# Attention with a token and channel mixer, one core: the product with the values in 64x64 tiles, its key halves added on VectorE, the first queries turned on TensorE, the order table refitted

## The chip, the cores and the metric

One core of a Trainium2 chip runs the kernel. The metric is the device time of one execution in microseconds (us). The clock that the throttle granted to TensorE in the profiled execution was 1.00 of full speed throughout.

## The reference

Causal attention over 4 batches of 12 heads (448 positions, head width 64) feeds a mixer: a small network over the positions of each batch, then one over the channels.

```
scores = q k^T / sqrt(64), causal mask, softmax          # 4 x 12 heads of 448 x 448
x  = softmax @ v, heads side by side                      # 4 x 448 x 768
u  = x + (relu(x^T @ w_tok1) @ w_tok2)^T                  # 448 -> 256 -> 448 over positions
out = u + relu(u @ w_ch1) @ w_ch2                         # 768 -> 1536 -> 768 over channels
```

Everything is float32 in and out.

## The kernel before

The work is cut into 24 pairs of heads, 0 to 23, six to a batch. For each pair the kernel loads keys, queries and values (`load_pair`), turns keys and queries so that the head width lies on the partitions (`prep`), makes the scores and the softmax (`heads`), turns the probabilities so that keys lie on the partitions, multiplies them with the values (`values`) and leaves the result, channels on partitions, in the tile `u`. After every second pair `xturn` turns two slices of `u` for the token network (`tokens`: lines L1350 and L1383); after every batch the channel network follows (`channels`, L1433). The last two batches take the channel network in combined products (L1765, L1836, L1860), 200 us that the change leaves alone.

**Two kinds of pairs.** Pairs 0 to 9 have their probabilities turned by TensorE (`by_tensor`, L1115); they are called flat here. For pairs 10 to 23 a DMA turns them (`by_dma`).

**The product with the values**, `values`, is three TensorE jobs. Two `pv` jobs (L1245) multiply blocks of 128 keys, in float32: the stationary side is 128 keys by 64 channels of one head (the array in two tiles of 128x64, one for each head of the pair), the moving side the probabilities. A `tips` job (L1254) takes the blocks on the causal diagonal that have only 64 keys; it uses the array as four tiles of 64x64, two halves of the keys by two heads. The queries are in seven chunks of 64; some chunks are gathered in the PSUM bank `ps`, the others in the bank `low`, and `evac` copies both parts to `u` (192 + 256 columns). The scores (L1021) use four 64x64 tiles as well.

**First pair.** Keys and queries of pair 0 come in blocks of 32x32 (four DMAs each, keys on SP's queue, queries on ACT's, L940) and VectorE turns both (L988). Pairs 1 to 5 come as they lie (`load_rows`, L892 and L895) and TensorE turns them by products with the identity (`turn_rows`, L916, L910); ACT or VectorE copies the result from PSUM.

**What sets the order.** Each piece of work is a job with a cost for each engine that may run it. A planner that runs while the program is built hands jobs to the engines one after the other: it takes the ready job with the lowest number in the table `PLACES`; `CHOICE` says which engine takes a job that several could do (a ACT, d VectorE, p GpSimd, s SP). Each engine then runs its list in this fixed order. Where TensorE has nothing ready in the plan early on, the planner puts in a filler product (`keep_warm`, L865), whose result nobody reads.

Of the kernel before, what the change touches and what calls it, by code (L numbers as in the profile page):

```python
# [9 lines left out]
F32 = mybir.dt.float32  # L10
# [11 lines left out]
    "load_pair.blocks": {-2: (0, 1), 10: (129, 153), 12: (193, 224), 14: (242, 259), 16: (338, 293), 18: (405, 420),  # L22
        20: (522, 537), 22: (578, 591), 24: (670, 694), 26: (742, 758), 28: (831, 851), 30: (911, 927), 32: (996,
        1006), 34: (1056, 1070), 36: (1141, 1151), 38: (1205, 1220), 40: (1280, 1293), 42: (1333, 1348), 44: (1406,
        1426)},
    "load_pair.load": {0.5: (2,), 2.5: (3,), 4.5: (178,), 6.5: (209,), 8.5: (274,), 10.5: (312,), 12.5: (393,),
        14.5: (453,), 16.5: (490,), 18.5: (558,), 20.5: (615,), 22.5: (704,), 24.5: (773,), 26.5: (822,), 28.5:
        (902,), 30.5: (949,), 32.5: (1047,), 34.5: (1114,), 36.5: (1194,), 38.5: (1241,), 40.5: (1376,), 42.5:
        (1441,), 44.5: (1489,), 46.5: (1531,)},
    "load_pair.upper": {-0.2: (12,), 1.8: (15,), 3.8: (213,), 5.8: (245,), 7.8: (317,), 9.8: (380,), 11.8: (441,),  # L30
        13.8: (505,), 15.8: (519,), 17.8: (592,), 19.8: (651,), 21.8: (727,), 23.8: (821,), 25.8: (859,), 27.8:
        (938,), 29.8: (982,), 31.8: (1077,), 33.8: (1136,), 35.8: (1226,), 37.8: (1269,), 39.8: (1401,), 41.8:
        (1462,), 43.8: (1517,), 45.8: (1561,)},
    "narrow.load": {3.5: (6, 9, 16, 62, 86, 121, 114, 144), 12: (288,), 13: (371,), 14: (445,), 15: (503,), 16:
        (606,), 17: (665,), 18: (755,), 19: (818,), 20: (897,), 21: (974,), 22: (1041,), 23: (1120,), 24: (1191,),
        25: (1254,), 26: (1328,), 27: (1400,), 28: (1463,), 29: (1511,), 30: (1553,), 31: (1599,), 32: (1627,), 33:
        (1660,), 34: (1687,), 35: (1730,)},
    "narrow.size": {3.5: (32, 52, 61, 116, 133, 177, 180, 235), 12: (352,), 13: (413,), 14: (484,), 15: (545,), 16:
        (642,), 17: (705,), 18: (786,), 19: (854,), 20: (932,), 21: (1013,), 22: (1072,), 23: (1153,), 24: (1223,),
        25: (1291,), 26: (1360,), 27: (1437,), 28: (1497,), 29: (1532,), 30: (1584,), 31: (1616,), 32: (1646,), 33:  # L40
        (1676,), 34: (1712,), 35: (1748,)},
    "narrow.shift": {3.5: (37, 56, 73, 125, 142, 183, 186, 263), 12: (359,), 13: (424,), 14: (491,), 15: (554,), 16:
        (646,), 17: (710,), 18: (793,), 19: (863,), 20: (939,), 21: (1019,), 22: (1084,), 23: (1157,), 24: (1227,),
        25: (1295,), 26: (1371,), 27: (1446,), 28: (1503,), 29: (1538,), 30: (1588,), 31: (1621,), 32: (1649,), 33:
        (1678,), 34: (1720,), 35: (1750,)},
    "narrow.join": {3.5: (40, 63, 80, 131, 146, 187, 194, 298), 12: (364,), 13: (436,), 14: (497,), 15: (587,), 16:
        (652,), 17: (724,), 18: (796,), 19: (870,), 20: (948,), 21: (1024,), 22: (1089,), 23: (1161,), 24: (1234,),
        25: (1300,), 26: (1374,), 27: (1450,), 28: (1505,), 29: (1543,), 30: (1590,), 31: (1623,), 32: (1655,), 33:
        (1681,), 34: (1725,), 35: (1755,)},
    "token_weights.<lambda>": {3.5: (44, 69, 85, 135, 150, 191, 201, 303)},  # L50
# [1927 lines left out]
```

## Time and profile before

| what | value |
|---|---|
| runs (3) | 537.52, 537.71, 538.35 us; median 537.71 |
| profiled execution | 538.04 us, of it span 536.2 us |
| TensorE, VectorE, ACT, GpSimd busy | 99%, 80%, 59%, 31% of the span |

The span runs from the first to the last instruction in the trace; 1.84 us of the profiled execution's time lie around it. PE is TensorE's row of products, PEld its loads of the stationary side, DVE is VectorE, POOL is GpSimd. In PE's rows the duration of a product includes its way through the array, so it overlaps with the next one: what a block of products costs is read from the start of its first row to the start of the block behind it. A float32 product shows as two records, so a block of 16 products is "x32" where rows are merged.

### The profile page before, as it was taken

The page shows a single profiled execution, that of the slowest core. Times are in us where ns is not written, and L with a number is a line of the kernel's source. Part 1 is how long each engine was busy: PE and PEld are TensorE (multiplying, and loading weights), DVE is VectorE, ACT ScalarE, POOL GpSimd, SP SyncE. Part 2 cuts the span into 40 slices and gives each one's busy share as a digit, 9 for nine tenths or more (in the row PEclk, how much of TensorE's full clock was granted, in tenths as well). Part 3 has the DMA queues.
Part 4 walks back from the last instruction along what each step waited for, and adds up shares of the span by engine and source line. Part 5 has one row for each costly group of instructions (what it writes and reads, how often), then busy time and mean ns, then how long its engine had stood idle before and what let it go on. Part 6 is the DMA issues. An engine that isn't in the chain of part 4 may idle for free.

```text
span 536.2 us, 12037 instructions
## 1 busy us (share of the span) xinstructions
PE 529.8 (99%) x4391; PEld 460.6 (86%) x4391; DVE 426.4 (80%) x1030; ACT 314.0 (59%) x768; POOL 164.2 (31%) x220
## 2 busy tenths in 40 slices
PE   8999999999999999999999999999999999999997
PEld 4778888888888888888898899999999999999996
DVE  5998899989797999888896679677877848485665
ACT  4998898899888787789784561243232313131300
POOL 2565745444252232332452132140010012321200
PEclk9999999999999999999999999999999999999999
DMA  9966677979999998999969327648213030212147
GB/s 194 198 116 144 152 214 160 215 153 233 207 178 200 225 190 193 205 196 229 210 163 198 115 92 205 131 119 162 88 32 116 7 91 23 87 32 88 31 75 131
DMA packets 221546, 77.72 MB, mean 145 GB/s; under 512 B 195760, under 2 KB 210992, under 8 KB 221488
## 3 DMA queue, kind: packets, MB, share of 16 engines
q1 hardware_dynamic: 207984, 74.90, 63.1%
q10 hardware_dynamic: 13504, 2.07, 2.1%
q8 instruction: 34, 0.56, 0.5%
q14 instruction: 24, 0.20, 0.2%
HBM read 49.15 MB, written 14.94 MB: 120 GB/s over the span
## 4 chain that ended last, share of the span: by engine, by line
PE 94%; SPq 2%; DVE 2%; ACT 1%; DMA 1%; issue 0%; POOL 0%; DVEq 0%; POOLq 0%
PE ps L1433 33%; PE ps L1860 16%; PE ps L1765 12%; PE ps L1021 6%; PE ps L1245 6%; PE ps L1383 6%; PE ps L1350 6%; PE ps L1836 3%; PE ps L1254 1%; PE ps L1115 1%; PE ps L1291 1%; SPq L940 1%; PE ps L865 1%; ACT prob L1055 1%; DMA gh<-in_k_dram 1%; PE ps L910 0%
## 5 line engine op out<-in xcount | busy, mean ns | idle before, releaser
L1500 DVE TENSOR_TENSOR u<-ps,u 128x448 f32<-128x448 f32 x118 | 72.5, 619 | 34.2 <-PE ps L1860 28.0
L1055 ACT ACTIVATE prob<-prob,stat 128x192 f32<-128x192 f32 (+6 forms) x168 | 83.7, 501 | 14.4 <-DVE stat L1043 14.1
L643 POOL TENSOR_TENSOR wl<-wf,wh 128x768 fp32r<-128x768 f32 x26 | 49.5, 1904 | 94.4 <-ACT wh L632 59.4
L1043 DVE CUSTOM_DVE_ANT_0 prob<-ps,mask 128x128 f32<-128x128 f32 (+6 forms) x168 | 63.3, 415 | 7.3 <-PE ps L1021 6.9
L634 POOL TENSOR_SCALAR prob<-prob,stat 128x64 f32<-128x64 f32 (+6 forms) x80 | 43.8, 559 | 55.4 <-DVE stat L1077 42.9
L1433 PE MATMUL ps<-uh,wh 128*128 128x448 f32 x144 | 53.7, 373 | 0.0
L1433 PE MATMUL ps<-gh,wh 128*128 128x448 f32 x144 | 52.9, 367 | 0.0
L1433 PE MATMUL ps<-gh,wl 128*128 128x448 f32 x144 | 52.7, 366 | 0.0
L1433 PE MATMUL ps<-gl,wh 128*128 128x448 f32 x144 | 52.7, 366 | 0.0
L1433 PE MATMUL ps<-uh,wl 128*128 128x448 f32 x144 | 52.7, 366 | 0.0
L1433 PE MATMUL ps<-ul,wh 128*128 128x448 f32 x144 | 52.7, 366 | 0.0
L632 ACT ACTIVATE wh<-wf 128x768 fp32r<-128x768 f32 x27 | 22.5, 846 | 51.2 <-PE ps L1860 25.8
L1021 PE MATMUL ps<-kq,kq 64*64 64x64 f32 (+5 forms) x768 | 45.4, 356 | 0.0
L1021 PEld LDWEIGHTS ps<-kq,kq 64*64 64x64 f32 x768 | 26.6, 133 | 15.5 <-issue 9.6
L1245 PE MATMUL ps<-pt,vraw 128*64 128x128 f32 (+2 forms) x544 | 37.3, 284 | 0.0
L1245 PEld LDWEIGHTS ps<-pt,vraw 128*64 128x64 f32 x544 | 28.2, 137 | 9.8 <-issue 2.1
L1795 DVE TENSOR_TENSOR kq<-kq,ps 128x448 f32<-128x448 f32 x35 | 21.2, 619 | 14.8 <-PE ps L1765 14.2
L1055 ACT ACTIVATION_READ_ACCUMULATOR prob<-prob,stat 128x1 f32 x168 | 32.1, 191 | 0.0
L638 ACT COPY pt<-pt 128x384 uint16<-128x384 uint16 (+3 forms) x41 | 31.6, 830 | 0.8 <-DMA pt<-prob 0.8
L1860 PE MATMUL ps<-u,wh 128*128 128x448 f32 (+1 forms) x110 | 31.0, 363 | 0.0
L1433 PEld LDWEIGHTS ps<-uh,wh 128*128 128x128 f32 x144 | 27.0, 188 | 2.8 <-issue 0.2
L1433 PEld LDWEIGHTS ps<-gl,wh 128*128 128x128 f32 x144 | 27.1, 188 | 2.5 <-DVE gl L1468 0.2
(222 smaller groups left out, 1403.2 us busy)
## 6 DMA issues: line engine op xcount, KB each, us to landing
wraw<-in_moe_w_ch_dram SPq DMA_DIRECT2D x24, 768.0 KB, 5.4
wf<-scratch SPq DMA_DIRECT2D x30, 384.0 KB, 3.1
scratch<-wf SPq DMA_DIRECT2D x24, 384.0 KB, 4.8
vraw<-in_v_dram SPq DMA_DIRECT2D x44, 96.0 KB, 3.4
kq<-in_k_dram SPq DMA_DIRECT2D x60, 56.0 KB, 3.7
kq<-in_q_dram SPq DMA_DIRECT2D x56, 56.0 KB, 2.4
out_dram<-h1l SPq DMA_DIRECT2D x24, 56.0 KB, 2.7
out_dram<-h1h SPq DMA_DIRECT2D x24, 56.0 KB, 2.2
```

Of the source, the lines that this page charges most:

```text
L634: eng[e].tensor_scalar(dst, src, scale, 0.0, op0=ALU.mult, op1=ALU.add)
L643: eng[e].tensor_tensor(dst, a, b, op=ALU.subtract)
L1021: nc.tensor.matmul(scores[n].tile[lanes, to:at], lhsT=qe.tile[LANES[j], c * QC:(c + 1) * QC], rhs=ke.tile[LANES[j], slice(*keys)], start=T ...
L1043: nc.vector.tensor_tensor_reduce(out=part(c, r), in0=ps.tile[:, at:at + wide(c)], in1=mask[:, S - QC:S + P] if c == 2 else mask[:, S - wid ...
L1055: nc.scalar.activation(part(c, r), part(c, r), AF.Exp, bias=stat.tile[:, 0, AT[c]:AT[c] + 1], scale=-1.0, accum_out=stat.tile[:, 1, AT[c]: ...
L1245: nc.tensor.matmul(to, lhsT=s.tile[:, kb, j], rhs=rhs, start=(n in first_of), stop=False)
L1350: nc.tensor.matmul(ps.tile[:, :PART], lhsT=w[:, c, m * P:(m + 1) * P], rhs=x.tile[:, c, :], start=(n == 0), stop=(n == len(work) - 1),)
L1383: nc.tensor.matmul(ps.tile[:, :S], lhsT=h.tile[:, m, o * P:(o + 1) * P], rhs=w[:, m, :], start=(n == 0), stop=(n == 3 * NM - 1),)
L1433: nc.tensor.matmul(ps.tile[:, :S], lhsT=x.tile[:, at_:at_ + P], rhs=y, start=(n == 0 and i == 0), stop=(n + 1 == w[2] and i == 2),)
L1500: eng[e].tensor_tensor(u, ps.tile[:, :S], u, op=ALU.add)
L1765: nc.tensor.matmul(ps.tile[:, :S], lhsT=l()[:, t * P:(t + 1) * P], rhs=r, start=(t == 0 and n == 0), stop=(t == half - 1 and n == 2),)
L1860: nc.tensor.matmul(ps.tile[:, cols], lhsT=l.tile[:, t * P:(t + 1) * P], rhs=r.tile[:, cols], start=(n == 0), stop=(n == 3 * len(fs) - 1),)
```

## The change

1. `values`: each block of 128 keys is split into two halves of 64 keys. All products of this stage now use four 64x64 tiles (two key halves by two heads); the half decides the PSUM bank: keys 0 to 63 add up in `ps`, keys 64 to 127 in `low`. The tips join the second `pv` job. A pair has twice as many products, each with half the depth.
2. `evac`: `nought` copies the whole of `low` (448 columns) to `u`, on ACT or VectorE; then `evac` adds the last 384 columns of `ps` to it, on VectorE.
3. The queries of pair 0 come as they lie, in one DMA of 224 KB on ACT's queue, and are turned on TensorE and copied by ACT or VectorE; VectorE turns only the keys of pair 0.
4. `PLACES` and `CHOICE` have new numbers throughout; two lines of each side stand below.

```
-    "load_rows.load": {0: (7, 4), 2: (10, 23), 4: (30, 45), 6: (68, 79), 8: (105, 91)},
+    "load_rows.load": {-2: (0,), 0: (3, 4), 2: (6, 17), 4: (20, 33), 6: (43, 114), 8: (103, 123)},
-    "load_pair.blocks": {10: "ss", 12: "ss", 14: "ss", 16: "ss"},
+    "load_pair.blocks": {10: "as", 12: "ss", 14: "ss", 16: "ss"},
...
-            {"sp": 535.0 if g < ONCE else 1070.0}, load, holds=[home, s], rank=2.0 * g + RL,
+            {"sp" if g else "act": 535.0 if g < ONCE else 1070.0}, load, holds=[home, s], rank=2.0 * g + RL,
...
+    def lies(g, nm):
+        return nm != "v" and g < WHOLE and (g, nm) != (0, "k")
...
-            if 0 < g < WHOLE and nm != "v":
+            if lies(g, nm):
...
-        def chunks(n, j):
+        def chunks(n, j, half):
 
             if flat_:
-                which, kb, c, step, nq, o, stride = PIECES[n]
-                out = banks[which].tile[LANES[j]].rearrange("p (c q) -> p c q", q=QC)[:, c:c + step * (nq - 1) + 1:step]
-                rhs = pt.tile[:, 1 - j if c in OVER else j, o:o + stride * (nq - 1) + 1:stride]
+                _, kb, c, step, nq, o, stride = PIECES[n]
+                out = banks[half].tile[LANES[j]].rearrange("p (c q) -> p c q", q=QC)[:, c:c + step * (nq - 1) + 1:step]
+                rhs = pt.tile[LANES[half], 1 - j if c in OVER else j, o:o + stride * (nq - 1) + 1:stride]
...
                 for n in part:
-                    for j in range(2):
-                        kb, to, rhs = chunks(n, j)
-                        nc.tensor.matmul(to, lhsT=s.tile[:, kb, j], rhs=rhs, start=(n in first_of), stop=False)
+                    for half in range(2):
+                        for j in range(2):
+                            kb, to, rhs = chunks(n, j, half)
+                            nc.tensor.matmul(to, lhsT=s.tile[LANES[half], kb, j], rhs=rhs, start=n == 0, stop=False)
+                for half, kb, o, c in ENDS if part[0] else ():
...
-                {"pe": 660.0 if part[0] else 718.0}, pv, js + pdone + [prev], [ps, low, s, ends, pt, u], rank, tiled=1
+                {"pe": 878.0 if part[0] else 652.0}, pv, js + pdone + [prev], [ps, low, s, ends, pt, u], rank, tiled=2
...
-        def evac(e):
+        def nought(e):
             if t == 0:
                 make(u, [P, NT, S], F32)
-            copy(e, u.tile[:, t, 3 * QC:], ps.tile[:, 3 * QC:S])
-            copy(e, u.tile[:, t, :3 * QC], low.tile[:, :3 * QC])
+            copy(e, u.tile[:, t], low.tile[:, :S])
+
+        def evac(e):
+            nc.vector.tensor_tensor(u.tile[:, t, QC:], ps.tile[:, QC:S], u.tile[:, t, QC:], op=ALU.add)
...
-        u_ready[b, t] = plan.job(
-            {"act": act_ps(S) + 65.0, "dve": dve1(S) + 70.0}, evac, [prev] + first, [ps, low, u], rank
-        )
+        c = plan.job({"act": act_ps(S), "dve": dve1(S)}, nought, [prev] + first, [low, u], rank)
+        u_ready[b, t] = plan.job({"dve": dve1(S - QC)}, evac, [prev, c], [ps, u], rank)
```

**TensorE's start, before.** After 16 fillers the list goes straight to the scores of pair 0 (L1021); the row behind them turns queries of pair 1 (L916).

```order
L865 MATMUL ps_84<-mask 128x512
L1021 MATMUL ps_140<-kq_121,kq_132 64x448 x2
L1021 MATMUL ps_141<-kq_121,kq_132 64x384 x2
L1021 MATMUL ps_141<-kq_121,kq_132 64x64 x2
L1021 MATMUL ps_149<-kq_121,kq_132 64x320 x2
L1021 MATMUL ps_150<-kq_121,kq_132 64x256 x2
...
L1021 MATMUL ps_149<-kq_121,kq_132 64x128 x2
L916 MATMUL ps_168<-ident,ul_118 64x112 x8
```

The same place in the changed kernel, where the turns are L914, the scores L1022 and the fillers L863. Between the sixth filler and the scores stand the turn of pair 0's queries and three more fillers.

```order
L863 MATMUL ps_84<-mask 128x512
L914 MATMUL ps_116<-ident,ul_96 64x112 x8
...
L863 MATMUL ps_84<-mask 128x512
L1022 MATMUL ps_133<-kq_126,kq_129 64x448 x2
L1022 MATMUL ps_134<-kq_126,kq_129 64x384 x2
...
L1022 MATMUL ps_147<-kq_126,kq_129 64x128 x2
L914 MATMUL ps_161<-ident,uh_113 64x112 x8
L914 MATMUL ps_178<-ident,ul_96 64x112 x8
L914 MATMUL ps_194<-ident,uh_113 64x112 x8
L1022 MATMUL ps_213<-kq_203,kq_206 64x448 x2
```

The first scores now wait for a product and a copy of it, nine fillers instead of 16 stand ahead of them, and three turns without a filler follow.

**TensorE around the values of pair 15, before** (`ps_3116` is the bank `ps`, `ps_3117` the bank `low`; then come scores of pair 17 and, with L1291, the turn of `u` for pairs 14 and 15).

```order
L1433 MATMUL ps_3099<-gh_3048,wl_3014 128x448
L1245 MATMUL ps_3116<-pt_3035,vraw_91 64x256 x2
L1245 MATMUL ps_3117<-pt_3035,vraw_91 64x128 x2
L1245 MATMUL ps_3116<-pt_3035,vraw_91 64x256 x2
L1245 MATMUL ps_3116<-pt_3035,vraw_91 64x128 x2
L1254 MATMUL ps_3116<-pt_3035,vraw_91 64x64 x2
L1254 MATMUL ps_3117<-pt_3035,vend_92 64x64 x2
...
L1021 MATMUL ps_3141<-kq_2941,kq_3005 64x448 x2
...
L1291 MATMUL ps_3169<-ident,u_2587 128x64
```

The same place in the changed kernel (L1247 the blocks, L1250 the tips, L1290 the turn of `u`; `ps_3310` is `ps`, `ps_3311` is `low`).

```order
L1432 MATMUL ps_3289<-gh_3130,wl_3182 128x448
L1247 MATMUL ps_3310<-pt_3200,vraw_91 64x256 x2
L1247 MATMUL ps_3311<-pt_3200,vraw_91 64x256 x2
L1247 MATMUL ps_3310<-pt_3200,vraw_91 64x128 x2
L1247 MATMUL ps_3311<-pt_3200,vraw_91 64x128 x2
...
L1250 MATMUL ps_3310<-pt_3200,vraw_91 64x64 x2
L1250 MATMUL ps_3311<-pt_3200,vend_92 64x64 x2
...
L1022 MATMUL ps_3338<-kq_3179,kq_3223 64x448 x2
...
L1290 MATMUL ps_3373<-ident,u_2786 128x64
```

Each row of the blocks now stands twice, once for each bank, and no row of this piece changes the tile shape between L1247 and the end of the scores.

**VectorE at the same place in the changed kernel** (L1266 is the new add; L1044 the masked scores of the next pair).

```order
L1499 TENSOR_TENSOR u_487<-ps_3289,u_487 128x448
L697 SCALAR_TENSOR_TENSOR wf_3302<-wraw_3219,wf_3302 128x768
L989 STREAM_TRANSPOSE kq_3351<-kq_3262 128x448
L1266 TENSOR_TENSOR u_2786<-ps_3310,u_2786 128x384
L1044 ISA prob_0_85,stat_3369<-ps_3338,mask 128x448
```

The add stands between work for other stages and the masked scores, which wait behind it.

## Rows read from the trace of the kernel before

**Rows 1.** The page, part 1: busy us (share of the span) x instructions.

```profile
PE 529.8 (99%) x4391; PEld 460.6 (86%) x4391; DVE 426.4 (80%) x1030; ACT 314.0 (59%) x768; POOL 164.2 (31%) x220
```

**Rows 2.** The page, part 4: the chain that ended last, by engine.

```profile
PE 94%; SPq 2%; DVE 2%; ACT 1%; DMA 1%; issue 0%; POOL 0%; DVEq 0%; POOLq 0%
```

**Rows 3.** Busy time by stretch: stretch, its length, PE, PEld, DVE, ACT, POOL, clock, DMA.

```profile
6.57:33.20 26.63, 25.83 (x438) 18.21 (x439) 24.75 (x101) 24.69 (x87) 14.34 (x32) 1.00 0.91 194
10.00:40.00 30.00, 29.28 (x523) 21.77 (x523) 28.41 (x113) 29.76 (x102) 18.22 (x41) 1.00 0.82 165
60.00:280.00 220.00, 220.00 (x2199) 187.63 (x2198) 197.56 (x554) 187.80 (x481) 84.80 (x112) 1.00 0.94 194
```

**Rows 4.** Fillers (L865) in the stretch 6.57 to 33.2 us: PE busy.

```profile
6.57:33.20 26.63, 3.65 (x12) 0.83 (x11) 1.00 0.91 194
```

**Rows 5.** Timeline of the start: start us, us, engine, line, operation [idle <-releaser].

```profile
0.71 2.05 ACTq L940 DMA_DIRECT2D kq<-in_q_dram  x4
...
4.94 1.17 DVE L988 STREAM_TRANSPOSE kq<-kq 128x448 f32<-128x448 f32 x2 [4.94 <-DMA kq<-in_k_dram]
...
5.31 1.28 ACT L1055 ACT_TABLE_LOAD   x1 [5.31 <-DMA vraw<-in_v_dram]
...
6.37 0.43 SPq L892 DMA_DIRECT2D uh<-in_k_dram  x1
...
6.57 1.79 PE L1021 MATMUL ps<-kq,kq 64*64 64x448 f32 x32
...
8.44 0.99 PE L916 MATMUL ps<-ident,ul 112*64 112x112 f32 x16
...
10.87 0.99 PE L916 MATMUL ps<-ident,uh 112*64 112x112 f32 x16 [0.68 <-DMA uh<-in_k_dram]
```

**Rows 6.** Timeline of PE: values between channel products and scores, pair 15.

```profile
178.01 0.37 PE L1433 MATMUL ps<-gh,wl 128*128 128x448 f32 x1
178.31 1.52 PE L1245 MATMUL ps<-pt,vraw 128*64 128x256 f32 x16
179.76 0.27 PE L1254 MATMUL ps<-pt,vraw 64*64 64x64 f32 x2
...
180.04 1.74 PE L1021 MATMUL ps<-kq,kq 64*64 64x448 f32 x32
181.71 0.71 PE L1291 MATMUL ps<-ident,u 64*128 64x64 f32 x16
```

**Rows 7.** Timeline of PE: tips of pair 22 ahead of token products.

```profile
285.38 0.27 PE L1254 MATMUL ps<-pt,vraw 64*64 64x64 f32 x2
...
285.78 0.68 PE L1383 MATMUL ps<-w2hi,h1h 128*128 128x448 f32 x2
```

**Rows 8.** Timeline of PE: tips inside a block of scores.

```profile
196.04 0.22 PE L1254 MATMUL ps<-pt,vraw 64*64 64x64 f32 x1
...
196.28 0.99 PE L1021 MATMUL ps<-kq,kq 64*64 64x256 f32 x20
```

**Rows 9.** Timeline of PE: values and turned probabilities of a flat pair.

```profile
27.34 1.56 PE L1245 MATMUL ps<-pt,vraw 128*64 128x128 f32 x32
28.83 0.27 PE L1254 MATMUL ps<-pt,vraw 64*64 64x64 f32 x2
...
29.22 0.65 PE L1115 MATMUL ps<-ident,prob 64*128 64x64 f32 x14
29.80 0.39 PE L865 MATMUL ps<-mask 128*128 128x512 bf16 x1
```

**Rows 10.** Groups of VectorE instructions by form: count | busy us, mean ns | idle before.

```profile
L1500 DVE TENSOR_TENSOR u<-ps,u 128x448 f32<-128x448 f32 x118 | 72.5, 619 | 34.2 <-PE ps L1860 28.0 <-PE ps L1433 4.7
...
L1887 DVE TENSOR_TENSOR u<-ps,u 128x224 f32<-128x224 f32 x4 | 1.5, 388 | 1.5 <-PE ps L1860 1.5
```

**Rows 11.** Groups of ACT instructions by form.

```profile
L632 ACT ACTIVATE pt<-ps 128x448 f32<-128x448 f32 x24 | 12.5, 533 | 0.0
```

**Rows 12.** Timeline after the tips of pair 15: the copies to u.

```profile
180.28 0.60 ACT L632 ACTIVATE u<-ps 128x256 f32<-128x256 f32 x2 [0.53 <-PE ps L1254]
```

More of the change, by code (lines that the diff above doesn't have):

```diff
@@ L21 @@
 PLACES = {
[L22 to L37, printed above, removed]
@@ new lines @@
+    "values.evac": {0: (144,), 2: (198,), 4: (252,), 6: (305,), 8: (375,), 10: (424,), 12: (492,), 14: (550,), 16:
+        (628,), 18: (663,), 20: (746,), 22: (805,), 24: (883,), 26: (965,), 28: (1039,), 30: (1094,), 32: (1174,),
+        34: (1253,), 36: (1324,), 38: (1378,), 40: (1459,), 42: (1546,), 44: (1595,), 46: (1639,)},
+    "xturn.turn": {1: (214,), 5: (329,), 9: (461,), 13: (582,), 17: (666,), 21: (810,), 25: (972,), 29: (1097,), 33:
+        (1261,), 37: (1381,), 41: (1581,), 45: (1646,)},
@@ L1226, in chunks @@
             view = pt.tile.rearrange("p o (j q) -> p o j q", j=2)
-            return kb, banks[c == 1].tile[LANES[j], c * QC:(c + nq) * QC], view[:, o, 1 - j if c in MIXED else j]
+            out = banks[half].tile[LANES[j], c * QC:(c + nq) * QC]
+            return kb, out, view[LANES[half], o, 1 - j if c in MIXED else j]
         def tip(o, c, j, half):
@@ L1247, in values @@
+                for half, kb, o, c in ENDS if part[0] else ():
+                    for j in range(2):
+                        nc.tensor.matmul(
+                            banks[half].tile[LANES[j], c * QC:(c + 1) * QC],
+                            lhsT=(ends if half else s).tile[LANES[half], kb, j], rhs=tip(o, c, j, half),
+                            start=False, stop=(o == 9),
+                        )
             prev = plan.job(
-                {"pe": 660.0 if part[0] else 718.0}, pv, js + pdone + [prev], [ps, low, s, ends, pt, u], rank, tiled=1
+                {"pe": 878.0 if part[0] else 652.0}, pv, js + pdone + [prev], [ps, low, s, ends, pt, u], rank, tiled=2
@@ L1249, in values @@
             )
-        def tips(e):
-            for half, kb, o, c in ENDS:
-                for j in range(2):
-                    nc.tensor.matmul(
-                        banks[half].tile[LANES[j], c * QC:(c + 1) * QC],
-                        lhsT=(ends if half else s).tile[LANES[half], kb, j], rhs=tip(o, c, j, half),
-                        start=False, stop=(o == 9),
-                    )
-        prev = plan.job({"pe": 282.0}, tips, [prev], [ps, low, s, ends, pt, u], rank, tiled=2)
```

292 lines of the change are left out of this document (146 added, 146 removed), and 205 rows, old and new, of tables (CHOICE, PLACES).

## The prediction

> **What bounds the kernel.** Four views, from coarse to fine. Part 1 of the page gives TensorE 99% of the span [rows 1]; that alone says little, since a product's duration overlaps the next. So second the chain that ended last: 94% of it is products [rows 2]. Third the busy time by stretch, which shows two regimes [rows 3]. From 60 to 280 us TensorE has no gap in 220 us, while VectorE is busy for 197.56 (90%) and ACT for 187.80 (85%): here only TensorE's own work counts. From 10 to 40 us ACT is busy for 29.76 of 30 and VectorE for 28.41: the softmax of the first pairs feeds too slowly, and TensorE's dense row holds fillers, 3.65 us in 12 records from 6.57 to 33.2 us [rows 4]. There TensorE time saved turns into waiting. Fourth TensorE's timeline, for what the product with the values costs.
>
> **TensorE's own part.** Pair 15 [rows 6]: blocks from 178.31 to 179.76 (1.45 us), tips to 180.04 (0.28), scores to 181.71 (1.67). The same tips cost 0.40 us (285.38 to 285.78) when token products follow [rows 7], against 0.28 ahead of scores: leaving a tile shape costs about 0.11 us. So 1.45 is 1.34 of work and one change of shape, and the stage works for 1.34 + 0.28 = 1.62 us. In a flat pair blocks take 1.49 and tips 0.39 with the change behind them [rows 9], that is 1.38 + 0.28 = 1.66.
>
> What replaces it has a row. Over both heads the scores of a pair stream 2 x (448 + 384 + 320 + 256 + 192 + 128 + 64) = 3584 columns through 64x64 tiles; the new stage streams 3072 for the blocks and 8 x 64 = 512 for the tips, 3584 too, in the same shape, on two banks at a time as well. Scores cost 1.67 less a change of shape behind them, 1.56 [rows 6]. Pairs 10 to 23 go from 1.62 to about 1.55, 0.07 less. Flat pairs have shorter products, half of them 64 columns wide. Sixteen such records took 0.24 us inside a block of scores, 196.04 to 196.28 [rows 8], so 0.06 for a round of four tiles. A flat pair has twelve such rounds (0.72) and eight of 128 columns, taken at twice the 0.053 that the scores' rate gives (1.56 x 128 / 3584) and a little more, 0.11: 1.62 in all, between 1.55 (the rate of the scores) and 1.68 (all at 0.06 for 64 columns). That is 0.04 less than 1.66.
>
> I count pairs 3 to 23, those behind the last filler: 14 x 0.07 + 7 x 0.04 = 1.3 us. The second part is changes of shape. Before, every pair changed once between blocks and tips, and once more where it met scores. In the lists from the first token product on I count 96 changes before and 84 after (the refitted table puts some new ones in by splitting scores): 12 x 0.11 = 1.3 us. Together 2.6 us. All other products stand in the lists in the same numbers.
>
> **The start.** VectorE no longer turns pair 0's queries: of its 1.17 us behind the keys' arrival at 4.94 half goes. But the first scores now wait for a chain: queries land, a turn (0.99 us, as for pair 1), a copy (0.53 [rows 11]), scores. If the queries land at 4.94 too, that is 6.5 or a little more with the hand-overs, against 6.57 [rows 5]. One DMA of 224 KB replaces four on ACT, and behind it ACT now issues keys of pair 6 ahead of the table load (1.28 us). That load is done before the turn is; if the four issues held it up, all of the 1.28 would show. I take 0 for the first scores, from -0.6 (VectorE's half) to +1.3. Next come three turns without a filler between them; their rows come over SP's queue, where k of pair 1 was issued at 6.37 and waited for until 10.87 [rows 5], so about 1 us of waiting can fall there, beside ACT's exponentials and hidden by them as long as ACT has pair 0 to work on. The list puts 16 fillers behind the first scores, where 11 stood: at 3.65 / 12 = 0.30 each the plan sees 1.5 us more of an idle TensorE. Against it ACT, which leads there, has 0.60 - 0.53 = 0.07 less to copy for each pair [rows 11, 12], and its list a little less to do early. I take +0.4 for the whole start, between -0.6 and +2.8 (1.3 + 1.5).
>
> **VectorE.** The add is new: 384 columns out of PSUM. The same operation took 619 ns for 448 columns and 388 for 224 [rows 10], so 388 + 231 x 160 / 224 = 553 ns, 13.3 us for 24 pairs. VectorE's idle time between 60 and 280 us is 22.4 us; 17 or so adds take 9.4 of it, unless the refitted choices move other work to ACT and GpSimd (84.80 of 220). In the queue the masked scores of the next pair stand behind the add, ACT's exponentials behind those. What hides it is the order: the turn of `u` for pairs 14 and 15 has a block of scores between it and the tips. Before, the copies started at 180.28 and took 0.60 [rows 12]; now 0.53 and 0.55 in a row end at 181.4 with a hand-over, 0.3 before TensorE gets there (181.71). I price it at 0; without that cover the late 0.55 would fall on TensorE.
>
> The Trainium skill, TensorEngine Tiling, section Performance Considerations, speaks against the change: tiling speeds up TensorE but not the emptying of PSUM, which may become the limit. The rows at 60 to 280 us have 10% of VectorE left, so by them it does not; by the rule the second rival below would hold.
>
> **Sum.** -1.3 - 1.3 + 0.4 = -2.2 us. The profiled execution took 538.04 us, of it 536.2 span, so 534.0 and 535.8; the median lies 0.33 below the profiled one: 535.5.
>
> **The rivals.** *The start gives it back.* If every added filler and the wait for the three turns reach the end (+1.5 and +0.8), 2.6 of gain leaves 0.3: 537.4, the same. For it: ACT and VectorE lead until 40 us, and the list has later fillers than before. Against: fillers are put where the plan idles, and ACT is not busier by them.
>
> *VectorE becomes the bound, slower.* If the adds come late, the masked scores behind them are late, then the exponentials, and TensorE waits. With 9.4 us more VectorE reaches 94% in that stretch; it decides once the remaining 13 us of idle time lie at the wrong places. If a third of the 21 pairs put 0.55 on TensorE, 3.9 us outweigh the 2.2; if all do, 11.6 - 2.2 = 9.4 is lost. A middle, two thirds, gives 7.7 - 2.2: 543. Against it: at 90% it made TensorE wait nowhere.
>
> *The many small products do not overlap, slower.* In the flat pairs 80 records stand where 48 stood. Turned probabilities, also 64 columns wide, took 0.58 us for 14 [rows 9], 41 ns each; at that rate 80 take 3.3 us instead of 1.66, 1.6 x 7 = 11.5 lost, less 2.3 of other gains, and the start's 0.4 on top: 547. Midway, at 28 ns, 80 records take 2.2 us, and the total is about 540. Against it: the tips, the very shape, ran at 15 ns a record in the middle of other work [rows 8]; at 15 ns 80 records take 1.2 us, below the 1.62 that the columns take. The Trainium skill, TensorE: Matmul & The Clock Gate, section on the 56 ns, says that two products never start less than about 25 ns apart. By that rule an estimate for 80 records is 2.0 us, 0.34 more than before in each of seven pairs, so 2.4 lost against 2.3 gained and the start's 0.4, near 538.2; the trace disagrees here, with its 15 ns.
>
> *No overlap of the halves at all*, 1.34 more for each of 21 pairs, 28 us: the scores run in four tiles at the rate used here, so I leave it 1 in 100.
>
> **How the numbers follow.** The forecast has 0.62, the start's rival 0.21, VectorE's 0.12, small products 0.04 (half of it for the form midway or milder), no overlap 0.01. 0.2% is 1.1 us, about what a measurement of this kernel can tell from no change: faster is below 536.6, same up to 538.8. The forecast case spans 534.0 (the start at -0.6 instead of +0.4, flat pairs at the scores' rate, 0.5 better) to 536.6. A part of the start's case ends just below 536.6, so faster is 0.65, same 0.20, slower 0.15. The range runs from 533.3, with 0.7 for what the new order may give that no row prices, to 539.0, which takes in the start's whole case and the mild end of VectorE's.
>
> **What would show it.** In the changed profile: values of a late pair, blocks and tips, in 1.5 to 1.6 us, of a flat one in 1.55 to 1.7; no 0.11 between them; TensorE still without a gap from 60 to 280 us; VectorE near 91 to 94% there; the add at 0.55 us; the first scores between 6.0 and 7.0 us. A wait of TensorE for the add or for masked scores beyond 1 us in sum, or more than 6 us of fillers behind the first scores, would make it wrong.

## The result, and the profile after

| kernel | median us | executions | range us |
|---|---|---|---|
| before | 537.62 | 20 | 536.83 to 539.80 |
| after | 540.44 | 20 | 539.07 to 543.56 |

After over before is 1.006, with a 95% interval of 1.0049 to 1.0072: slower by 2.8 us, where 2.2 us faster was forecast. The profiled execution of the changed kernel is its quickest one, 539.07 us with a span of 536.9; the profile of before had 538.04 and 536.2. So of the 2.8 us the two traces show 0.7 in the span and 1.0 in the time; the rest is what other executions of the changed kernel lose against the profiled one (the median lies 1.4 above it), while before's profiled execution lay 0.4 above its median.

The page of the changed kernel, part 1 (as [rows 1]: busy us, share, instructions) and the engines of part 4 (as [rows 2]):

```profile
PE 530.2 (99%) x4949; PEld 462.2 (86%) x4949; DVE 433.8 (81%) x1045; ACT 316.1 (59%) x752; POOL 163.0 (30%) x221
...
PE 91%; DMA 4%; ACT 1%; DVE 1%; SPq 1%; issue 0%; DVEq 0%
```

TensorE is still the chain, with 4% for transfers where there was 1%. The stretches of [rows 3], after:

```profile
10.00:40.00 30.00, 29.36 (x600) 20.82 (x597) 28.95 (x114) 29.03 (x98) 17.94 (x41) 1.00 0.81 174
60.00:280.00 220.00, 219.67 (x2562) 187.59 (x2553) 198.81 (x565) 191.40 (x472) 87.52 (x122) 1.00 0.91 195
```

From 60 to 280 us TensorE is busy for 219.67 of 220, as the forecast had it, and VectorE for 198.81 (90%, forecast 91 to 94). From 10 to 40 us VectorE now stands at 28.95 of 30. TensorE's timeline gives the stage itself, first a late pair, then a flat one, each with the block behind it (as [rows 6, 9]):

```profile
178.78 1.53 PE L1247 MATMUL ps<-pt,vraw 64*64 64x256 f32 x32
180.13 0.22 PE L1250 MATMUL ps<-pt,vraw 64*64 64x64 f32 x2
...
180.36 1.74 PE L1022 MATMUL ps<-kq,kq 64*64 64x448 f32 x32
...
42.08 1.57 PE L1247 MATMUL ps<-pt,vraw 64*64 64x128 f32 x64
43.47 0.23 PE L1250 MATMUL ps<-pt,vraw 64*64 64x64 f32 x2
43.48 0.22 PE L1250 MATMUL ps<-pt,vend 64*64 64x64 f32 x2
43.53 0.22 PE L1250 MATMUL ps<-pt,vraw 64*64 64x64 f32 x2
...
43.81 0.39 PE L1349 MATMUL ps<-xh,w1hi 128*128 128x256 f32 x1
```

178.78 to 180.36 is 1.58 us with a change of shape ahead (forecast 1.55, or 1.5 to 1.6); 42.08 to 43.81 is 1.73 with one behind (1.62 without the 0.11). The add and the copy of `low`, groups of instructions by form:

```profile
L1266 DVE TENSOR_TENSOR u<-ps,u 128x384 f32<-128x384 f32 x24 | 13.1, 546 | 0.4 <-ACT u L630 0.3
...
L630 ACT ACTIVATE u<-ps 128x448 f32<-128x448 f32 x20 | 10.8, 538 | 3.9 <-PE ps L1250 3.6
```

546 ns and 13.1 us in all (forecast 553 and 13.3). What TensorE waited for, the longest first (us in total, times, longest):

```profile
PE ps L863 <- POOL mask L648: 1.5, 1, 1.5
PE ps L908 <- DMA uh<-in_k_dram: 0.5, 1, 0.5
PE ps L1432 <- DVE wl L641: 0.4, 1, 0.4
PE ps L1290 <- DVE u L1266: 0.3, 1, 0.3
```

One wait of 0.3 us for the add. So nearly all the signs that the prediction named are there, those that were to make it wrong are absent, and it is wrong all the same. Where TensorE's time went is seen when its timeline is added up by what a block is, each block from its start to the start of the next:

| block | before us | after us | difference |
|---|---|---|---|
| values and tips | 42.82 | 39.85 | -2.97 |
| channel products (L1433, L1432) | 178.58 | 180.06 | +1.48 |
| second token product (L1383, L1382) | 30.69 | 31.32 | +0.63 |
| turn of `u` (L1291, L1290) | 7.57 | 8.12 | +0.55 |
| turn of keys and queries as they lie | 6.60 | 8.77 | +2.17 |
| fillers | 9.02 | 8.08 | -0.94 |
| scores | 42.57 | 42.76 | +0.19 |
| all others | 215.02 | 214.37 | -0.65 |

The row of values gave more than was forecast for it and all changes of shape together (2.97 against 2.6). The next three rows take back 2.66 and the scores 0.19, and their products are the same in number. What is left of the 2.6 is 0.1.

The start (as [rows 5]), timeline:

```profile
0.71 0.43 ACTq L890 DMA_DIRECT2D ul<-in_q_dram  x1
...
4.17 1.76 PE L914 MATMUL ps<-ident,ul 112*64 112x112 f32 x16
...
5.98 0.54 ACT L630 ACTIVATE kq<-ps 128x448 f32<-128x448 f32 x1 [1.29 <-PE ps L914]
...
7.09 1.79 PE L1022 MATMUL ps<-kq,kq 64*64 64x448 f32 x32
```

The queries land before 4.17, but their turn takes 1.76 us where the same turn took 0.99 later on [rows 5], and the first scores come at 7.09 instead of 6.57. TensorE is slow there as a whole: the three fillers behind the turn stand 0.4 us apart, in before fillers did so up to 4.46 us and stood 0.21 apart behind it. The profile gives the granted clock as 1.00 in both stretches, so it does not show why.

### The profile page after: what moved, and what is told of

Its sections match the earlier page's. It is cut to its first block, busy times and chain, and to the rows that moved or that the text cites. A ratio compares the mean times of both kernels' runs of the same rounds, so it can differ in the third digit from the quotient of the medians.

```text
span 536.9 us, 13133 instructions
## 1 busy us (share of the span) xinstructions
PE 530.2 (99%) x4949; PEld 462.2 (86%) x4949; DVE 433.8 (81%) x1045; ACT 316.1 (59%) x752; POOL 163.0 (30%) x221
## 4 chain that ended last, share of the span: by engine, by line
PE 91%; DMA 4%; ACT 1%; DVE 1%; SPq 1%; issue 0%; DVEq 0%
PE ps L1432 31%; PE ps L1859 16%; PE ps L1764 12%; PE ps L1022 7%; PE ps L1247 6%; PE ps L1349 6%; PE ps L1382 5%; PE ps L1835 3%; PE ps L1116 2%; PE ps L1290 1%; DMA pt<-prob 1%; PE ps L1250 1%; DMA wraw<-in_moe_w_ch_dram 1%; DMA vraw<-in_v_dram 1%; DMA uh<-in_k_dram 1%; PE ps L863 1%
## 5 line engine op out<-in xcount | busy, mean ns | idle before, releaser
L1056 ACT ACTIVATE prob<-prob,stat 128x256 f32<-128x256 f32 (+6 forms) x168 | 83.9, 502 | 13.6 <-DVE stat L1044 11.1
L641 POOL TENSOR_TENSOR wl<-wf,wh 128x768 fp32r<-128x768 f32 x22 | 42.1, 1915 | 107.7 <-ACT wh L630 95.8
L1044 DVE CUSTOM_DVE_ANT_0 prob<-ps,mask 128x64 f32<-128x64 f32 (+6 forms) x168 | 63.8, 414 | 5.9 <-PE ps L1022 4.9
L632 POOL TENSOR_SCALAR prob<-prob,stat 128x64 f32<-128x64 f32 (+6 forms) x82 | 46.2, 572 | 38.7 <-DVE stat L1078 35.1
L1432 PE MATMUL ps<-uh,wh 128*128 128x448 f32 x144 | 53.8, 373 | 0.0
L1432 PE MATMUL ps<-gh,wh 128*128 128x448 f32 x144 | 53.3, 370 | 0.0
L1432 PE MATMUL ps<-gh,wl 128*128 128x448 f32 x144 | 52.7, 366 | 0.4 <-DVE wl L641 0.4
L1432 PE MATMUL ps<-uh,wl 128*128 128x448 f32 x144 | 52.8, 366 | 0.0
L1432 PE MATMUL ps<-gl,wh 128*128 128x448 f32 x144 | 52.7, 366 | 0.0
L1432 PE MATMUL ps<-ul,wh 128*128 128x448 f32 x144 | 52.7, 366 | 0.0
L1022 PE MATMUL ps<-kq,kq 64*64 64x128 f32 (+5 forms) x768 | 47.1, 359 | 0.1
L1022 PEld LDWEIGHTS ps<-kq,kq 64*64 64x64 f32 x768 | 27.2, 133 | 19.6 <-issue 10.6
L1247 PE MATMUL ps<-pt,vraw 64*64 64x128 f32 (+2 forms) x1088 | 37.7, 279 | 0.0
L1247 PEld LDWEIGHTS ps<-pt,vraw 64*64 64x64 f32 x1088 | 31.1, 133 | 6.5 <-issue 1.5
L636 ACT COPY prob<-prob 128x768 uint16<-128x768 uint16 (+1 forms) x39 | 34.7, 919 | 0.1
L1432 PEld LDWEIGHTS ps<-uh,wh 128*128 128x128 f32 x144 | 27.0, 188 | 3.2 <-issue 0.5
L1432 PEld LDWEIGHTS ps<-gh,wl 128*128 128x128 f32 x144 | 27.0, 188 | 2.9 <-DVE wl L641 0.7
```

The source lines that it names most:

```text
L632: eng[e].tensor_scalar(dst, src, scale, 0.0, op0=ALU.mult, op1=ALU.add)
L636: nc.scalar.copy(out, in_)
L641: eng[e].tensor_tensor(dst, a, b, op=ALU.subtract)
L1022: nc.tensor.matmul(scores[n].tile[lanes, to:at], lhsT=qe.tile[LANES[j], c * QC:(c + 1) * QC], rhs=ke.tile[LANES[j], slice(*keys)], start=T ...
L1044: nc.vector.tensor_tensor_reduce(out=part(c, r), in0=ps.tile[:, at:at + wide(c)], in1=mask[:, S - QC:S + P] if c == 2 else mask[:, S - wid ...
L1056: nc.scalar.activation(part(c, r), part(c, r), AF.Exp, bias=stat.tile[:, 0, AT[c]:AT[c] + 1], scale=-1.0, accum_out=stat.tile[:, 1, AT[c]: ...
```

## The experiments

Each kernel ran in some 4 to 12 executions beside before on the same chip; ratios are to before. Kernels of different groups ran on different chips, so across groups the ratios are the safer measure. The tables name pairs by twice their number, with an offset for loads and turns: 20 is pair 10 under `values`, pair 11 under `load_pair.blocks`, and 18.5 under `load_pair.load` is pair 9.

**Parts alone, the planner free.** First each part was undone or done alone, the planner making a new order each time. The values stage in before, with the numbers of the old `evac` for the copy and half a step more for the add:

```
-    "values.evac": {0: (143,), 2: (203,), 4: (238,), 6: (309,), 8: (406,), 10: (452,), 12: (498,), 14: (555,),
...
+    'values.evac': {0: (143.5,), 2: (203.5,), 4: (238.5,), 6: (309.5,), 8: (406.5,), 10: (452.5,), 12: (498.5,),
...
+    'values.nought': {0: (143,), 2: (203,), 4: (238,), 6: (309,), 8: (406,), 10: (452,), 12: (498,), 14: (555,),
...
```

> The product with the values in 64x64 tiles with its add, in the order table of the kernel before (the add directly behind the copy); first queries as before. Theory A (the new stage is worth about 3 us, the loss of the change comes from the refitted order and the start): 534 to 536 us, values and tips of a late pair near 1.55 us. Theory B (the add on VectorE takes the gain back): 537.5 us or more, with waits of TensorE for the add or for masked scores above 1 us in sum.

Measured: 549.39 us, 1.0205 (1.018 to 1.0231).

The changed kernel with before's `values` (its diff reversed):

> The changed kernel with the product and the copies of before put back: refitted table and first queries without 64x64 tiles and without the add. Theory A: slower than the changed kernel by about 3 us, 542 to 545. Theory B: faster than the changed kernel, 538 or less, since the add is gone.

Measured: 544.25, 1.0107 (1.0079 to 1.0135).

The changed kernel with the first queries as before:

```
-        return nm != "v" and g < WHOLE and (g, nm) != (0, "k")
+        return nm != "v" and 0 < g < WHOLE
```

> The changed kernel with pair 0's queries loaded in blocks and turned by VectorE as before. Theory C (the start is what was lost: first scores at 7.09 us and not 6.57): 0.5 to 1.5 us faster than the changed kernel, 539 to 540. Theory A puts the start at most at a part of the loss: 0 to 1 us faster; if the stalls behind are what counts, no difference, 540.4.

Measured: 548.93, 1.0191 (1.0158 to 1.0224).

Before with the first queries of the change:

> The kernel before with pair 0's queries loaded as they lie on ACT's queue and turned by TensorE, old table. Theory C: first scores 0.5 us later and the whole 0.5 us longer, 538.1. If the first softmax stages hide it: 537.6, the same.

Measured: 546.42, 1.0152 (1.0124 to 1.018).

All four lie 6 to 12 us above before, undoing as well as doing. So they price no part. With the order held (below), the first, third and last edit come out 1.0, 0.9 and 0.1% above before, where the planner had them at 2.1, 1.9 and 1.5; the second comes out the same either way (1.0 and 1.1%). An edit that makes the planner order anew, without a table fitted to it, can cost more than any term of the forecast.

**Parts alone, the order held.** From here on the order is written out: a list of all jobs with engine and PSUM banks, as the planner of one kernel had made it, replayed job for job.

```
+ORDER = [
+    ['F'],
...
+        for row in ORDER:
+            if row[0] == "F":
+                self.filler.fn("pe")
```

Before's order with the new stage: the tips go into the second `pv`, the copy takes the place of the old one, the add stands about 0.7 us behind it in the plan.

> Every engine's list exactly as in the kernel before, written out, with only the product with the values replaced: both jobs in 64x64 tiles, the copy of the whole bank in the place of the old copies, the add on VectorE 0.68 us of planned time behind it. Theory A (the stage itself gains about 3 us, what was lost came with the refitted lists): 534 to 536 us. Theory B (the add on VectorE takes it back): 537.5 or more, TensorE waits behind the add or the masked scores.

Measured: 543.65 us, 1.0103 (1.0079 to 1.0127). TensorE's waits from 8 to 305 us:

```profile
PE ps L3244 <- DVE u L3220: 4.5, 5, 2.0
PE ps L3070 <- DVE u L3220: 0.9, 2, 0.6
PE ps L2865 <- DVE wf L2650: 0.7, 1, 0.7
PE ps L3336 <- DVE u L3220: 0.5, 1, 0.5
```

L3220 is the add; L3244 the turn of `u`, L3070 the turn of probabilities, L3336 a token product: 5.9 us of waits for the add. So in the old order the add is on TensorE's way. The longest of the waits, 1.97 us at 130.56, costs about twice its length; the windows around it (length, PE busy, clock):

```profile
128.00:130.00 2.00, 0.59 (x16) 1.00 1.10 273
130.00:132.00 2.00, 1.44 (x11) 0.79 1.19 222
132.00:134.00 2.00, 2.00 (x7) 0.50 0.97 214
134.00:136.00 2.00, 2.00 (x10) 0.86 1.12 331
```

After a stretch in which TensorE was busy for 0.59 of 2 us the granted clock falls to 0.50, 1.2 GHz, for a while.

The refitted order with the old stage:

> Every list exactly as in the changed kernel, with the product of before (tips behind the second job, two copies in the place of the one, no add). Theory A: 3 us slower than the changed kernel, 543 to 544. Theory B: the same as the changed kernel or faster, 540.5 or less.

Measured: 544.08, 1.0104 (1.0086 to 1.0123), executions from 543.79 to 544.34. From 8 to 305 us TensorE's list of waits has one line, 0.6 us, and yet the kernel is 5.5 us slower than the 538.59 of before beside it. The order itself has a price, with this stage in it.

The refitted order with everything, replayed:

> The changed kernel with its lists written out instead of planned: the same instructions in the same order, so 540.4 us by every theory; its profile is a second look at where a slower execution than the profiled 539.07 loses time. Theory D (the new order meets DMA waits that vary from run to run): another set of waits for loads of weights, values or turned probabilities than in the first profile.

Measured: 541.19 (539.00 to 544.63), 1.0048 (1.0029 to 1.0067): as the changed kernel. In the refitted order the stage is worth 2.9 us (544.08 to 541.19). The profiled execution has a span of 539.6, 2.7 more than the profile above in the same order; up to 96 us the two run within 0.7 of one another, then 2.5 us are lost in one place. Its timeline there:

```profile
85.90 2.24 SPq L2897 DMA_DIRECT2D kq<-in_k_dram  x4
88.18 6.33 SPq L2897 DMA_DIRECT2D kq<-in_q_dram  x4
...
95.17 0.65 DVE L2945 STREAM_TRANSPOSE kq<-kq 128x448 f32<-128x448 f32 x1 [3.54 <-DMA kq<-in_k_dram]
...
96.72 0.55 DVE L3222 TENSOR_TENSOR u<-ps,u 128x384 f32<-128x384 f32 x1
...
98.88 0.68 DVE L2597 TENSOR_TENSOR xl<-ps,xh 128x512 fp32r<-128x512 f32 x1
...
99.70 0.44 PE L3388 MATMUL ps<-uh,wh 128*128 128x448 f32 x1 [1.34 <-DVE xl L2597]
```

VectorE stands for 3.54 us at the turn of pair 12's keys, which were issued from 85.90 on and have not landed; the add and the residue `xl` stand behind it in its list, and TensorE waits for them. In the quicker execution the same lists have this:

```profile
81.50 0.96 SPq L950 DMA_DIRECT2D vraw<-in_v_dram  x2
82.51 1.35 SPq L954 DMA_DIRECT2D vraw<-in_v_dram  x1
...
85.07 2.33 SPq L941 DMA_DIRECT2D kq<-in_k_dram  x4
87.45 4.81 SPq L941 DMA_DIRECT2D kq<-in_q_dram  x4
...
91.45 0.64 DVE L989 STREAM_TRANSPOSE kq<-kq 128x448 f32<-128x448 f32 x1
...
94.21 0.65 DVE L989 STREAM_TRANSPOSE kq<-kq 128x448 f32<-128x448 f32 x1 [0.65 <-DMA kq<-in_q_dram]
```

Here the turn of the same keys, at 91.45, waits for nothing, and the turn of the queries behind it for 0.65. The refitted `CHOICE` gives the three loads of values at 81.50 to SP, ahead of these keys; before had them on ACT's queue.

The refitted order with the first queries as before: six fillers stand for their turn.

> Every list exactly as in the changed kernel, but pair 0's queries come in blocks and are turned by VectorE, with 15 fillers ahead of the first scores. Theory C (the later first scores, 7.09 us and not 6.57, are carried to the end): about 0.5 us faster than the changed kernel, 539.9. If the stages behind hide it: 540.4.

Measured: 543.60, 1.0091 (1.0066 to 1.0116), with one wait of 3.4 us of scores for a copy of keys or queries. In an order fitted to it the new way of the queries is worth about 2.4 us.

**The add and the late keys.** The stage in the last 14 pairs alone, before's order, and their seven turns of `u`, with the copies behind them, moved behind one more product:

```
-    ['xturn.turn', 21.0, 0, 'pe', 6, 5],
...
+        (values_old if g < TURN else values_new)(g)
...
+    ['xturn.turn', 21.0, 0, 'pe', 6, 5],
```

> Before's order written out, the 64x64 stage in the last 14 pairs alone, and in those pairs the turn of u placed one more channel or token product later in TensorE's list (2 us). Theory 'the add's waits': in the old order with the new stage in all pairs the turn of u waited 4.5 us in 5 for the add; with the turns behind 2 us of products these waits go, the stage gives 14 times some 0.09 us and 14 changes of tile shape of 0.1 us, so 535.0 us (534.3 to 536.5) and no wait of the turn for the add over 0.5 us in sum. Theory 'VectorE is too long': the add pushes the masked scores behind it wherever the turn stands, so 538 us or more, with TensorE waiting for masked scores or for banks instead.

Measured: 538.02, 0.9996 (0.9985 to 1.0007): the number of the second theory, at its edge. But the turns wait no more, as the first had it; nothing is gained either, and the next runs take the moves apart.

The refitted order with those loads of values back on ACT's queue:

```
-    ['load_pair.load', 18.5, 0, 'sp'],
+    ['load_pair.load', 18.5, 0, 'act'],
```

> The refitted order with one job on another queue: the three loads of values of pair 9 are issued on ScalarE's queue, as in the kernel before, not on SP's ahead of the keys of pair 11. Theory 'late keys': in the slow executions of the refitted order VectorE stands for up to 3.5 us at the turn of these keys, with the add and the residues behind it; without the loads ahead the keys come 2.3 us sooner, the median falls from 541.2 (540.4 in the first comparison) to 539.3 and the executions lie closer together (within 2 us). Otherwise: 540.4 to 541.2 as before, spread over 4 us, or slower by the 2.4 us that ScalarE then spends on issuing.

(The keys are pair 12's.) Measured: 540.04, 1.0035 (1.0022 to 1.0047), executions from 539.08 to 541.18. Its 12 executions lie within 2.1 us, the replay's 12 within 5.6. The ratio falls by 0.13% against the replay, whose interval overlaps, and by 0.25%, or 1.3 us, against the changed kernel, whose interval begins just above. So the late keys are a part of the spread, and not the whole loss.

The add cut to one column, the sum over the other columns left out, in either order:

```
-            nc.vector.tensor_tensor(u.tile[:, t, QC:], ps.tile[:, QC:S], u.tile[:, t, QC:], op=ALU.add)
+            nc.vector.tensor_tensor(u.tile[:, t, QC:QC + 1], ps.tile[:, QC:QC + 1], u.tile[:, t, QC:QC + 1], op=ALU.add)
```

> Before's order with the new values stage in all pairs, and the add cut down to one column of 384 (the sum over the other columns is left out), with its place and its waits kept: this takes 24 times 0.5 us off VectorE and nothing off TensorE. Theory 'the add costs': of the 543.65 us with the whole add some 6 go, 537 to 538, and if its length is all that the old order lacks 534.5. Theory 'the old order does not fit the new stage otherwise' (ScalarE's copies, banks): 542 or more.

Measured: 541.22, 1.0054 (1.0034 to 1.0073).

> The refitted order with the add cut down to one column (the sum over the other columns is left out). Theory 'the order pays': the refitted order has taken the add off TensorE's path by moving the turns of u, so its length costs little here, 0.5 to 1.5 us, all of it in executions that come late: 539 to 540.5. Theory 'VectorE is the bound in the new order too': 3 us or more go, 538 or less.

Measured: 540.61, 1.0051 (1.0032 to 1.007).

The add's length is worth 2.4 us in the old order (543.65 less 541.22; 0.5% by the ratios), between the 6 of the first theory and the at most 1.6 of the second, and 0.6 or nothing in the refitted one (541.19 less 540.61; the ratios are 1.0048 and 1.0051). That the refitted order costs what it does because it hides the add is argued and not shown.

**Which pairs, and what a moved turn costs.** As the run with the late pairs, with three turns moved instead of seven:

> As the run with the late pairs alone (538.0), but of the seven turns of u only the three that had waited for the add in the old order are moved 2 us later. Theory 'a moved turn costs by itself': among 128-row products it takes one more change of tile shape, some 0.2 us, so four turns left in their place give back 0.8 us: 537.0 (536.2 to 537.7), under before. Theory 'VectorE is too long wherever the turn stands': 538 or more, with the four turns waiting again.

Measured: 536.99, 0.9978 (0.9964 to 0.9992), as the theory of the moved turn had it, under before.

Before's order and stage, the seven turns moved:

> Before's order and before's values stage, with the seven late turns of u moved 2 us later and nothing else. Theory 'a moved turn costs by itself': seven more changes of tile shape of about 0.2 us, 1.0 to 1.6 us, 539.0 to 539.5. Theory 'the place of a turn is free while TensorE has other work' (the price in the prediction): within 0.3 us of before.

Measured: 539.07, 1.002 (1.0007 to 1.0034): 1.2 us for seven by the medians, 0.17 each (0.4 to 1.8 us by the interval). A moved turn costs by itself. In the trace channel and token products are 1.6 us dearer than before's and the scores 0.9 cheaper.

The late pairs, no turn moved:

> The new stage in the late pairs alone and every turn of u where before had it. Theory 'the add's waits': the waits of the turn for the add come back, some 3.5 us in three, less the 2.2 us that the stage gives and the 1.4 us of the moved turns: about 538.5 (537.7 to 540). Theory 'the flat pairs are what hurts in the old order': no late wait over 1 us and 536 or less.

Measured: 536.59, 0.997 (0.9958 to 0.9983): quicker than before and after, nearer to the second theory, and not told apart from the run with three turns moved. Its waits of the turn for the add:

```profile
PE ps L3315 <- DVE u L3288: 1.1, 2, 0.9
```

Before's order with the new way of the first queries:

```
-    ['load_pair.blocks', -2.0, 1, 'act'],
+    ['load_rows.load', -2.0, 0, 'act'],
...
-    ['F'],
+    ['turn_rows.turn', -1.5, 0, 'pe', 0],
+    ['turn_rows.evac', -1.5, 0, 'act'],
```

> Before's order with the first queries loaded as they lie and turned on TensorE in place of six fillers, nothing else. Theory 'the start pays': the turn at the lower clock is 1.7 us on TensorE in front of the first scores, which come near 7.1 us and not 6.57, and the stretch behind them is bound by VectorE and ScalarE, so 0.5 to 1.5 us slower: 538.3 to 539.3. The prediction's own price (+0.4): 538.1. If one turn fewer on VectorE makes the start shorter: 537.2 or less.

Measured: 538.57, 1.0007 (0.9994 to 1.002): no difference that can be told, 0.7 us by the medians. The first scores come at 6.87.

Then the first ten pairs alone, in before's order:

```
+        (values_new if g < TURN else values_old)(g)
```

> Before's order with the new stage in the first ten pairs alone. Theory 'VectorE and ScalarE set the pace there': ten adds of 0.55 us and the copies ahead of them fall on a stretch that has no room, so 5 us or more slower than before, 542.5 to 545, with TensorE waiting for masked scores, the add or banks up to 100 us. Theory 'only both parts together hurt' (lateness from the first ten meets the late turns): under 540.

Measured: 542.56, 1.0108 (1.0073 to 1.0143). TensorE's waits from 8 to 100 us:

```profile
PE ps L3070 <- DVE u L3288: 1.6, 3, 0.6
PE ps L3315 <- DVE u L3288: 0.9, 2, 0.7
PE ps L3407 <- DVE u L3288: 0.8, 1, 0.8
```

All three wait for the add: turned probabilities, the turn of `u`, a token product, 3.3 us in sum. Of it 1.2 falls before 40 us (at 25.5, 32.8 and 37.6) and 2.0 later (at 47.5, 68.7 and 85.1). The ten pairs by themselves cost 5.1 us, the 14 gain 1.3; both together lost 5.1 and not 3.8. That difference of 1.3 is no more than the intervals allow (1.9 us either way for the ten pairs alone).

> The refitted order with the old stage in the first ten pairs and the new one in the last 14. Theory 'the refitted order made room for the first ten adds': TensorE gets back ten times some 0.15 us of slower stage and about ten changes of tile shape of 0.1, so 1 to 2.5 us slower than with the new stage in all pairs (541.2 and 540.4): 542 to 543. Theory 'it still pays for them': the ten adds gone, 539.5 or less.

Measured: 540.32, 1.0048 (1.0032 to 1.0064), the same as with the new stage in all pairs (541.19 and 540.44), between the two theories: in the refitted order those ten pairs neither gain nor cost.

## Why the prediction was wrong

**The stage: the total was met by luck.** Forecast -2.6 with all changes of shape, the new ones elsewhere too; the row of values has -2.97, but only with the changes that it lost. Pair for pair the stage did what was said: 0.15 us less in the same surroundings, from 1.73 [rows 6] to 1.58 in a late pair and from 1.88 [rows 9] to 1.73 in a flat one, where the forecast had 0.18 and 0.15. The trace shows no sign of products that do not overlap: 42.08 to 43.81 holds 80 records, and a float32 product shows as two records, so 1.62 us for 80 are 40 ns for a product. The rule of the Trainium skill (TensorE: Matmul & The Clock Gate, section on the 56 ns) is that no two products start less than about 25 ns apart. On the mean these 40 ns and the tips' 30 ns of [rows 8] keep to it, and the prediction had set 15 ns for a record against it. But within a round of four tiles the rows do not keep to it: tips start two and two at 43.47 and 43.48, the next ones at 43.53.

**The price of a change of shape: this is the step that failed.** That "leaving a tile shape costs about 0.11 us" was read where the tips end [rows 7], and with it the prediction worked out both terms of its 2.6: the 1.34 us of work in the blocks, from which it had 1.3 less work in 21 pairs, and 12 x 0.11 for the lists. The rows give more for a stay in a shape, its change in and its change out. First, from before, a flat pair's blocks in two halves:

```profile
61.29 0.89 PE L1245 MATMUL ps<-pt,vraw 128*64 128x128 f32 x16
62.11 1.09 PE L1115 MATMUL ps<-ident,prob 64*128 64x64 f32 x28
63.13 0.89 PE L1245 MATMUL ps<-pt,vraw 128*64 128x128 f32 x16
63.95 1.79 PE L1021 MATMUL ps<-kq,kq 64*64 64x448 f32 x32
```

They take 0.82 and 0.82, in one piece 1.49 [rows 9]: 0.15 for a stay in 128x64. From the changed kernel, late values and a block of scores each between 128-row products, and the channel products behind scores:

```profile
74.83 1.79 PE L1022 MATMUL ps<-kq,kq 64*64 64x448 f32 x32
76.55 0.39 PE L1349 MATMUL ps<-xh,w1hi 128*128 128x256 f32 x1
...
97.02 0.47 PE L1432 MATMUL ps<-uh,wh 128*128 128x448 f32 x1
97.33 0.37 PE L1432 MATMUL ps<-ul,wh 128*128 128x448 f32 x1
...
182.03 0.71 PE L1290 MATMUL ps<-ident,u 64*128 64x64 f32 x16
...
288.26 1.53 PE L1247 MATMUL ps<-pt,vraw 64*64 64x256 f32 x32
...
289.95 0.67 PE L1382 MATMUL ps<-w2hi,h1h 128*128 128x448 f32 x2
```

Apart they take 1.69 and 1.72, together 3.25 (178.78 to 182.03): 0.16 for a stay in 64x64. A channel product takes 0.20, but 0.31 behind scores (97.02 to 97.33) and 0.30 ahead of a turn (100.61 to 100.91, below): 0.20 for a stay in 128x128. By these the old stage works for 1.45 - 0.15 + 0.39 - 0.16 = 1.53 us in a late pair and 1.57 in a flat one, and so does the new one, 1.69 - 0.16 and 1.73 - 0.16: the 1.3 us of less work were not there. All that the new stage saves is stays, and the refitted order puts other ones in. Counted in the two traces:

| shape | stays before | after | price | us |
|---|---|---|---|---|
| 128x64 | 26 | 0 | 0.15 | -3.9 |
| 64x64 | 37 | 43 | 0.16 | +1.0 |
| 128x128 | 39 | 47 | 0.20 | +1.6 |
| 64x128 | 25 | 28 | 0.15 (taken as the first) | +0.5 |

That is -0.9, an estimate, where the forecast had -2.6. The waits for `wl` and for the add in the list above take 0.7 of it, and 0.2 is left; the rows of the first table give 0.1. The count of changes itself was right (137 to 127 in all, 99 to 87 from the first token product on). With the new stage in before's order it is 112: the refit puts 15 back.

**The add at nothing: right in the changed kernel, wrong in the old order.** The sentence "I price it at 0" rested on the stretch from 60 to 280 us and on the order around pair 15. In the changed kernel it holds: one wait of 0.3 us, and 0.6 or nothing from cutting the add. In the old order it holds for the last 14 pairs, which alone make the kernel 0.3% quicker with no turn moved (536.59), and fails for the first ten, which alone make it 5.1 us slower (542.56 against 537.47). The stretch from 10 to 40 us, where [rows 3] show VectorE at 28.41 of 30, was read as one where TensorE time saved turns into waiting; that VectorE time spent there turns into waiting as well was left out. But only a third of the waits for the add fall there. The others lie between 47 and 85 us, where before's VectorE is busy for 85 to 94%, as it is from 100 to 140 us (37.56 of 40), among the pairs that gain. So what sets the ten pairs apart is not shown. Nor is the add's length the whole: only 2.4 us hang on it in the old order. That the sum is a chain of two steps on two engines, where the copy was one, may explain the rest: in the run with the new stage in all pairs VectorE itself waited 3.8 us in five for ACT's copy. That was seen, not tested.

**The refitted order: not free.** Three things were left out.

First, it keeps TensorE from waiting for the add (0.3 us) by putting the turns of `u` further behind the values, between products that were one block before. A turn between channel products, timeline of the changed kernel:

```profile
100.61 0.37 PE L1432 MATMUL ps<-uh,wl 128*128 128x448 f32 x1
100.91 0.71 PE L1290 MATMUL ps<-ident,u 64*128 64x64 f32 x16
101.55 0.39 PE L1349 MATMUL ps<-xh,w1hi 128*128 128x256 f32 x1
```

Channel products start 0.20 us apart; the turn starts 0.30 behind the last one. Before, such a turn stood behind scores [rows 6], and the step from scores to 128-row products had to be taken in any case. Seven turns so moved, with the copies behind them, cost before's kernel 1.2 us. The Trainium skill, TensorEngine Tiling, section Tiling Modes, says that a change of mode drains TensorE; the runs agree, with 0.17 us for each moved turn. Blocks of scores that stand alone between 128-row products cost in the same way.

Second, the new stage in the first ten pairs is worth nothing in that order: 540.32 without it, 540.44 and 541.19 with it. That what TensorE saves there is spent on the add's way is a guess.

Third, the order runs closer to its transfers. VectorE's list has the turn of pair 12's keys ahead of an add, and SP's list has loads of values ahead of these keys; where they come late, 2.5 us are lost at once. The old stage in the same order, 1.3 us later at that place, had its six executions within 0.6 us of one another.

**The start: +0.4 was low.** The turn of the queries took 1.76 us, not 0.99, and the first scores came 0.52 later, within the bounds given. By the table the turns of keys and queries cost 2.17 more and fillers 0.94 less, 1.2 in all. Held in before's order this part costs 0.7 us by the medians, which is not told from nothing.

**What stays open.** The 0.1 that is left of the stage's gain, the 1.2 of the start and 0.65 less in all other rows leave the changed kernel 0.5 us slower in the table, and 0.7 in the spans. The larger part of the 2.8 us lies between executions, and the runs do not say what share of the changed kernel's 1.4 us between its quickest execution and the median is the late keys. The refitted order with the old stage is 5.5 us slower than before, and its trace has no wait to show for it. In it the trace counts 166 changes of shape against 137; the stays come to 5.1 us by the prices above, the first turns give 2.2 and fillers take back 0.8, 6.5 in all, an estimate too large by 1.

## What to carry to other kernels

Price a change of tile shape on both sides: not only the block that is left behind but also the first and the last product of its neighbours, and count which shapes an order adds, not only the net. Here that made 0.15 to 0.20 us for each stay in a shape, where 0.11 was read. An order fitted to one set of durations has a price of its own when a stage is exchanged: hold it and change one part, since letting the planner order anew made three of four edits here 5 to 8 us dearer than they are with the order held. An added instruction of 0.55 us was free in 14 pairs and not in ten; the busy share of its engine did not tell which, the waits in the trace did. And a stage that is better in one half of its calls is used there: the late pairs alone, in the old order, gave the only versions here that beat both kernels.

## What the runs showed of the hardware that was not expected

A wait of TensorE can cost more than its length: behind a wait of 1.97 us the granted clock went from 1.00 to 0.50 in one stretch of 2 us, and token products started 0.75 us apart instead of 0.41. A stall of 2.5 us in another run (0.66 of 2 us busy from 98 to 100 us) left the clock at 1.00. And the four loads of pair 12's queries took 2.78 us to issue on SP's queue in before, 4.81 in the changed kernel's profile and 6.33 in its replay; those of pair 11's took 4.59, 2.75 and 2.81, so it is not the order alone.
